# Second feed-forward product from split float32r operands, tail convolutions on VectorE

## The chip, the core and the metric

One core of a Trainium2 chip runs the whole program. The metric is the device time of one execution in microseconds, as the median of several runs. A profile of one execution shows what each engine does: TensorE (PE for its matmuls, PEld for its weight loads), VectorE (DVE), ScalarE (ACT), GpSimd (POOL) and the queue that issues DMAs (SP). "L538" is line 538 of the kernel before.

## The reference

Top-32 attention over 8 batches, 8 heads, 576 positions of 64 values, then a gated feed-forward net with 512 inputs, 1024 hidden channels and 512 outputs:

```python
scores = scale * np.matmul(q, k.transpose(0, 1, 3, 2))
kth = np.partition(scores, -top_k, axis=-1)[..., -top_k:-top_k + 1]
scores = np.where(scores >= kth, scores, -1000000000.0)
attn = softmax(scores)                      # over the last axis
x = np.matmul(attn, v)                      # heads side by side: (8, 576, 512)
h = np.maximum(x @ w_in, 0.0)
for k in range(3):
    conv_out += conv_w[k] * hp[:, k:k + S]  # along the positions, zero at the ends
gate = 1.0 / (1.0 + np.exp(-conv_out))
out = (h * gate) @ w_out
```

The weights arrive as 64-bit floats and are turned into 32-bit values on the chip.

## The kernel before

The attention is cut into 288 row tiles: 8 batches, 4 pairs of heads, 9 tiles of 128 rows each. A software pipeline runs one turn (`iteration`) per row tile, so a batch takes 36 turns. In a turn TensorE transposes the weights of an older tile (L304), does a share of the feed-forward work, computes scores of a new tile (L212, L217, L220) and the product with v (L335, L338). ScalarE takes the signs against the threshold (`sides`, L266), evacuates scores (L226) and transposes (L309) and takes exponentials into PSUM (`expo`, L278). VectorE looks for the 32nd largest score (L233, L253, L255, L281, L285) and weighs (L291). GpSimd multiplies scores with signs (`flip`, L271) and has the convolutions. Inside the loop the order of instructions on each engine is the order in which the program text emits them; behind the loop (the drain) a scheduler orders them.

The feed-forward net of a batch runs while the next batch attends. Its 576 positions are two parts, 256 and 320 rows. An `Expand` is one of 8 slices of 128 hidden channels of one part: 12 float32r matmuls (L400: high by high, high by low, low by high, for 4 slices of the input), a relu on ScalarE (L411), the convolution in two steps on GpSimd (`conv_a`, `conv_b`: L430, L439, L444), a tanh on ScalarE (L458), a gate on VectorE (L466). Each slice of hidden channels has a tile of its own (`g0_0` to `g1_7`). In the drain every second expansion of the last part has its convolution on VectorE (`conv_v`, L450).

A `Contract` is the second product of one block of up to 128 rows: 8 float32 matmuls of 512 columns with the gated activations as weights (L538), and for the last 64 rows of a batch 16 of 256 columns whose two halves go to different output partitions (L545). ScalarE copies the result to a tile `o` (L554, L557) and a DMA takes it out. The last five full blocks (the 320-row part of batch 6, and batch 7) instead use float32r: `halve` (L514 on ScalarE, L515 on VectorE) makes high and low parts of w_out and of the activations, and 24 float32r matmuls of 512 columns do the product (L534). Those pieces lie in `spare` and in tiles that the attention no longer needs.

A planner decides how much of it goes into a turn. `FEED` microseconds of planned TensorE time are added to a credit per turn, at most `PE_CAP`; `run_units` takes units from the two lanes, expansions first, until the credit is gone. A new expansion starts every `PACE` = 2 turns, and not while a contraction of the same part of an older batch is still queued. GpSimd tasks wait in a queue, `pool_tasks`, with planned costs and 2.0 us per turn.

At the start 33 blocks of weights are converted, one per turn: VectorE L148, L149, L159, ScalarE L153 to L155, GpSimd L164 and then L168 to L170 for w_in (which is split into a high and a low part) or L166 alone for w_out. Temporary tiles come from the tags of five groups of activation tiles.

## Time and profile before

| what | value |
|---|---|
| median of 3 runs | 1182.77 us (1179.51 to 1186.13) |
| the profiled execution | 1178.58 us, span 1176.8 us |
| TensorE | 1073.1 us busy, 91% of the span |
| VectorE | 1064.6 us, 90% |
| ScalarE | 973.8 us, 83% |
| GpSimd | 853.5 us, 73% |
| mean granted TensorE clock | 0.968 of full speed |
| chain of waits, by engine | TensorE 72%, VectorE 20%, ScalarE 5% |

Busy time is the union of an engine's instructions. A share of the whole span mixes three stages: a start in which weights are converted (to about 160 us), the loop, and the drain from about 1100 us. What a change is worth is read from the stage in which it lies. The chain of waits is followed back from the last instruction: each piece is what released the next one.

### The profile page before, as it was taken

How to read it: one execution, taken by the hardware profiler on the slowest of the kernel's cores; microseconds unless marked ns; L12 is line 12 of the kernel's file. 1: busy time of each engine (PE TensorE's matmuls, PEld its weight loads, DVE VectorE, ACT ScalarE, POOL GpSimd, SP SyncE). 2: the span in 40 equal slices, each digit the busy share in tenths (PEclk: the TensorE clock that was granted, in tenths of full speed). 3: DMA queues.
4: the chain of work that ended last, by engine and by line, in shares of the span. 5: the costliest groups of instructions: out<-in, count | busy, mean ns of one | idle time of the engine just before them, and what ended most of it. 6: DMA issues, size and time to landing. Idle time of an engine off the chain costs nothing.

```text
span 1176.8 us, 27192 instructions
## 1 busy us (share of the span) xinstructions
PE 1073.1 (91%) x7922; PEld 722.1 (61%) x7922; DVE 1064.6 (90%) x5823; ACT 973.8 (83%) x2295; POOL 853.5 (73%) x1147
## 2 busy tenths in 40 slices
PE   3666666889999999999999999999999999999997
PEld 1333444666666666666666665666666666666785
DVE  7999999999999999999999999999999999999451
ACT  5778888998988888898989888888988898898451
POOL 6776665778767786777767786877767886877770
PEclk9976689999999999999999999999999999999998
DMA  6230111111101111111110111111111011110001
GB/s 237 77 96 12 44 46 45 45 46 45 52 23 53 50 54 54 54 57 56 54 47 26 43 53 54 55 58 54 54 54 50 20 45 54 54 36 20 29 14 44
DMA packets 52095, 60.75 MB, mean 52 GB/s; under 512 B 9664, under 2 KB 31456, under 8 KB 51936
## 3 DMA queue, kind: packets, MB, share of 16 engines
q1 hardware_dynamic: 51936, 58.91, 15.9%
q8 instruction: 65, 1.06, 0.4%
q14 instruction: 94, 0.77, 0.2%
HBM read 49.31 MB, written 9.58 MB: 50 GB/s over the span
## 4 chain that ended last, share of the span: by engine, by line
PE 72%; DVE 20%; ACT 5%; POOL 1%; issue 1%; DMA 1%; SPq 0%; ACTq 0%; DVEq 0%; POOLq 0%
PE me L400 14%; PE mc L538 14%; PE s_ps L335 10%; PE pt L304 9%; PE s_ps L217 9%; DVE cand L233 5%; PE s_ps L220 3%; DVE e L291 3%; DVE z L281 3%; PE s_ps L212 3%; PE mc L545 2%; DVE cv L159 2%; PE s_ps L338 2%; DVE cand L255 1%; PE mc L534 1%; PE weights_ps L534 1%
## 5 line engine op out<-in xcount | busy, mean ns | idle before, releaser
L271 POOL TENSOR_TENSOR z<-rows,side 128x579 f32<-128x579 f32 x288 | 348.1, 1209 | 234.6 <-ACT side L266 217.4
L233 DVE MAX8 cand<-rows 128x8 f32<-128x82 f32 (+1 forms) x2016 | 453.0, 239 | 0.0
L278 ACT ACTIVATE weights_ps<-rows,z 128x576 f32<-128x576 f32 x288 | 219.6, 762 | 38.0 <-DVE e L291 29.7
L226 ACT COPY rows<-s_ps 128x576 f32<-128x576 f32 x288 | 183.0, 635 | 63.8 <-PE s_ps L338 41.9
L291 DVE SCALAR_TENSOR_TENSOR e<-rows,kth,weights_ps 128x576 f32<-128x576 f32 x288 | 230.6, 801 | 0.2
L266 ACT ACTIVATE side<-rows 128x576 bf16<-128x576 f32 x288 | 223.2, 775 | 0.9 <-DVE rows L253 0.7
L400 PE MATMUL me<-x_hi,wi 128*128 128x322 f32 (+1 forms) x928 | 220.1, 310 | 0.0
L281 DVE MAX8 z<-z 128x8 f32<-128x576 f32 x288 | 214.1, 744 | 0.0
L217 PE MATMUL s_ps<-k,q 64*128 64x512 f32 x512 | 157.8, 695 | 48.1 <-ACT xt L346 34.2
L304 PE MATMUL pt<-ident,e 128*128 128x128 f32 x1152 | 190.1, 290 | 10.9 <-DVE e L291 9.1
L538 PE MATMUL mc<-wo,g 128*128 128x512 f32 x416 | 198.8, 593 | 0.0
L335 PE MATMUL s_ps<-pT,vn 128*64 128x128 f32 (+1 forms) x2560 | 167.3, 275 | 17.5 <-ACT rows L226 17.5
L335 PEld LDWEIGHTS s_ps<-pT,vn 128*64 128x64 f32 x2560 | 131.0, 140 | 71.7 <-ACT rows L226 23.6
L400 PEld LDWEIGHTS me<-x_hi,wi 128*128 128x128 f32 x928 | 158.0, 190 | 0.9 <-issue 0.4
L304 PEld LDWEIGHTS pt<-ident,e 128*128 128x128 f32 x1152 | 134.1, 147 | 36.7 <-issue 19.4
L309 ACT COPY pT<-pt 128x512 f32<-128x512 f32 x256 | 151.5, 592 | 2.1 <-PE pt L304 2.1
L430 POOL TENSOR_SCALAR t<-g,cr 128x256 f32<-128x256 f32 (+1 forms) x248 | 129.7, 524 | 15.0 <-ACT g L411 13.9
L400 PE MATMUL me<-x_lo,wi 128*128 128x258 f32 (+1 forms) x464 | 137.7, 297 | 0.0
L253 DVE MAX8 rows<-cand 128x8 f32<-128x21 f32 x576 | 109.7, 190 | 0.0
L285 DVE SCALAR_TENSOR_TENSOR hot<-weights_ps,cnt,z 128x10 f32<-128x10 f32 x288 | 63.0, 219 | 49.6 <-ACT weights_ps L458 38.3
L444 POOL TENSOR_TENSOR t<-t,t 128x256 f32<-128x256 f32 (+1 forms) x124 | 99.8, 805 | 9.7
L220 PEld LDWEIGHTS s_ps<-k,q 128*128 128x128 f32 x256 | 40.9, 201 | 107.4 <-issue 107.4
(208 smaller groups left out, 1758.6 us busy)
## 6 DMA issues: line engine op xcount, KB each, us to landing
k<-in_k_dram SPq DMA_DIRECT2D x32, 352.0 KB
q<-in_q_dram SPq DMA_DIRECT2D x32, 288.0 KB
vn<-in_v_main_dram SPq DMA_DIRECT2D x32, 256.0 KB
rb<-row SPq DMA_DIRECT2D x64, 128.0 KB
out_dram<-o SPq DMA_DIRECT2D x32, 256.0 KB
raw<-in_w_in_dram SPq DMA_DIRECT2D x16, 256.0 KB
raw<-in_w_out_dram SPq DMA_DIRECT2D x16, 256.0 KB
vt<-in_v_tail_dram SPq DMA_DIRECT2D x32, 64.0 KB
```

What stands on the lines that cost most here:

```text
L217: nc.tensor.matmul(s_ps[:, 2 * h * BANK:(2 * h + 1) * BANK], lhsT=qx[d, at], rhs=kx[d, h * TAIL:h * TAIL + MAIN], start=True, stop=True)
L226: nc.scalar.copy(out=x, in_=s_ps[:, at:at + S])
L233: yield lambda c=c, at=at, n=n: nc.vector.max(out=t.cand[:, c:8 * CHUNKS:CHUNKS], in_=t.x[:, at:at + n])
L266: nc.scalar.activation(out=t.side[:, 2:S + 2], in_=t.x, func=AF.Sign, scale=-OVER, bias=t.row[:, 7:8], accum_out=t.cnt)
L271: nc.gpsimd.tensor_tensor(t.z[:, 8:S + 11], t.row[:, 6:S + 9], t.side, ALU.mult)
L278: nc.scalar.activation(out=e_ps, in_=t.x, func=AF.Exp, scale=scale, bias=t.shift)
L281: nc.vector.max(out=t.z[:, 0:8], in_=t.z[:, 10:S + 10])
L291: nc.vector.scalar_tensor_tensor(out=t.e, in0=t.x, scalar=kth[:, t.n:t.n + 1], in1=e_ps, op0=ALU.is_ge, op1=ALU.mult, accum_out=t.pc.sums[ ...
L304: nc.tensor.transpose(tp[:, i * P:(i + 1) * P], t.e[:, o + i * P:o + (i + 1) * P], ident)
L335: nc.tensor.matmul(a[r, 0:w], lhsT=st.pc.vn[:, h, i], rhs=st.pT[:, h if st.i < NI else 1 - h, i, 0:w], start=(i == 0), stop=False)
L400: nc.tensor.matmul(mm[:, 0:w], lhsT=wt, rhs=xx, start=(n == 0), stop=(n == len(ops) - 1))
L538: nc.tensor.matmul(mm, lhsT=h[:, at + self.s0:at + self.s0 + self.m], rhs=wo[:, f], start=(f == 0), stop=(f == NFT - 1))
```

## The change

Every block of the second product is now computed in float32r, from a high and a low part of both operands: high by high, high by low, low by high, 24 matmuls of 512 columns per block. w_out is split once, while it is converted. The activations are split per half row block (four hidden slices of 128 rows, 512 columns; for the last 64 rows all eight slices at once): a copy to float32r on ScalarE, and one turn later a subtraction on GpSimd; in the drain on VectorE at once. The 64-row blocks no longer use two halves of the output partitions. All slices of a part share one tile `g`. Three split buffers take the place of the conversion's scratch tile, which has three sets instead of five. An expansion waits until all older blocks of its part are split, instead of multiplied. In the drain all convolutions are on VectorE. One output tile instead of two; FEED 1.42 for 1.56, PE_CAP 1.6 for 1.8. The pieces, `spare` and `halve` are gone.

```diff
-PE_CAP = 1.8
-FEED = 1.56
+PE_CAP = 1.6
+FEED = 1.42
-OB = 2
+OB = 1
-SPARES = 6
+SPB = 3
...
-            self.tags = [f"g{k % 2}_{k // 2}" for k in range(i % 5 * 3, i % 5 * 3 + 3)]
+            if not scratch:
+                scratch.append(moe.tile([P, 4 * SPB, WB], F32, name="scratch", tag="split"))
+            self.at = i % SPB * 4
...
-                yield Convert(w_out[f * P:(f + 1) * P, n:n + WB], P, wo[:, f, n:n + WB], None)
+                yield Convert(w_out[f * P:(f + 1) * P, n:n + WB], P, wo[:, 0, f, n:n + WB], wo[:, 1, f, n:n + WB])
...
-            h = self.h = moe.tile([P, ROWS[self.part][1] - ROWS[self.part][0] + 4], F32, name=f"g{self.part}_{self.f}")
...
+            if self.f == 0:
+                g = self.gs["g"] = moe.tile([P, NFT, n + 4], F32, name=f"g{self.part}")
...
-            if self.b == B - 1 and self.part == 1 and self.f % 2 == 0 and not exact:
+            if state.it > NT + 4 and not exact:
                 self.conv_v()
...
-            self.count = NFT
-            self.cost = NFT * 4 * (DM if halves is None else DM // 2) / 2400
+            nf = NFT * TAIL // self.m
+            self.fs = range(half * nf, half * nf + nf)
+            self.first, self.final, self.ready = half == 0, self.fs[-1] == NFT - 1, False
+            self.count = nf
+            self.cost = nf * 3 * (DM / 2400 + 0.012)
+
+        def split(self):
...
+            both = extra[state.split % len(extra)] if late else parts[0][:, state.split % SPB]
+            self.hi, self.lo = (both[:, i].rearrange("p (f m) -> p f m", m=self.m) for i in range(2))
...
+            src = self.gs["g"][:, self.fs[0]:self.fs[-1] + 1, c0:c0 + self.m]
...
+            nc.scalar.copy(out=self.hi, in_=src)
+
+            def rest(engine):
+                engine.tensor_tensor(self.lo, src, f32(self.hi), ALU.subtract)
+                self.ready = True
+                unready.remove(self)
+
+            if state.it > NT + 4:
+                rest(nc.vector)
+            else:
+                pool_tasks.append((state.it + 1, 1.3, lambda: rest(nc.gpsimd)))
...
+            for i, f in enumerate(self.fs):
+                for n, (x, e) in enumerate(((self.hi, 0), (self.hi, 1), (self.lo, 0))):
+                    start, stop = f + n == 0, f == NFT - 1 and n == 2
+                    nc.tensor.matmul(mm[0:m], lhsT=x[:, i], rhs=wo[:, e, f], start=start, stop=stop)
                 yield self.cost / self.count
...
+    def split_next():
+        if not unready or blocks or fetched or cut or acted or dved:
+            return False
+        c = next((c for c in unready if not hasattr(c, "hi")), None)
+        if c is None or c.gs.get("done", 0) < NFT or (state.late_splits >= 4 if state.it > NT + 4 else state.splits >= SPB):
+            return False
+        c.split()
+        return True
...
-        if any(o.part == e.part and o.b < e.b for o in contracts) or (state.it < state.due and not tail):
-            return None
-        if contracted.cur is not None and contracted.unit.part == e.part and contracted.left > LEFT:
+        if any(o.part == e.part and o.b < e.b for o in unready) or (state.it < state.due and not tail):
             return None
...
-    for f in range(NFT):
-        pair = piece(), piece()
-        halve(wo[:, f], *pair)
-        wo2.append(pair)
-    for e in unsplit:
-        e.halve()
...
-    wo = const.tile([P, DF // P, DM], F32, name="wo")
+    wo = const.tile([P, 2, DF // P, DM], F32R, name="wo")
```

`split_next` is called once per turn, right behind the relus and output copies at the head of the turn (in the drain as often as it finds something).

## Rows read from the trace of the kernel before

**Rows 1.** The page, busy tenths in 40 equal slices of the span.
```profile
PE   3666666889999999999999999999999999999997
DVE  7999999999999999999999999999999999999451
```
**Rows 2.** Busy time by stage: one batch, and 14 us of the loop.
```profile
core 0: us, PE busy (x) PEld busy (x) DVE busy (x) ACT busy (x) POOL busy (x), PEclk, DMA share, GB/s
430.20:560.40 130.20, 129.53 (x982) 85.83 (x981) 122.19 (x707) 115.11 (x272) 98.35 (x132) 1.00 0.16 50
...
623.27:637.29 14.02, 14.02 (x104) 9.36 (x104) 13.94 (x84) 12.00 (x29) 12.68 (x19) 1.00 0.01 2
```
**Rows 3.** The chain of waits from 300 to 1000 us, shares by line.
```profile
by line: PE mc L538 20.1%; PE me L400 19.3%; PE s_ps L335 13.8%; PE pt L304 13.0%; PE s_ps L217 12.1%; PE s_ps L220 4.8%; PE s_ps L212 3.4%; PE s_ps L338 2.9%; PE mc L545 2.8%; PE me L317 1.8%; ACT rows L226 1.2%; ACT side L266 1.1%; issue 
```
**Rows 4.** Groups by line, 265 to 1070 us (busy, mean ns | idle before), and one wait.
```profile
L271 POOL TENSOR_TENSOR z<-rows,side 128x579 f32<-128x579 f32 x222 | 267.3, 1204 | 165.0 <-ACT side L266 164.0
L226 ACT COPY rows<-s_ps 128x576 f32<-128x576 f32 x222 | 141.7, 638 | 55.5 <-PE s_ps L338 36.9 <-PE s_ps L220 17.2
L285 DVE SCALAR_TENSOR_TENSOR hot<-weights_ps,cnt,z 128x10 f32<-128x10 f32 x221 | 48.8, 221 | 48.0 <-ACT weights_ps L458 38.1 <-ACT weights_ps L278 8.7
...
620.14 0.23 DVE L285 SCALAR_TENSOR_TENSOR hot<-weights_ps,cnt,z 128x10 f32<-128x10 f32 x1 [1.48 <-ACT weights_ps L458]
```
**Rows 5.** The chain in order of time: start us, us, what (merged).
```profile
269.07 2.58 PE mc L538 x6
...
1153.88 4.84 PE weights_ps L534 x21
...
1164.97 3.63 PE weights_ps L545 x32
```
**Rows 6.** Groups by line over the whole span, second product.
```profile
L538 PE MATMUL mc<-wo,g 128*128 128x512 f32 x416 | 198.8, 593 | 0.0
...
L545 PE MATMUL mc<-wo,g 128*64 128x256 f32 x224 | 28.6, 388 | 0.0
```
**Rows 7.** Copies on ScalarE (timeline, group) and subtractions on GpSimd (groups).
```profile
1092.00 2.18 ACT L514 CAST rows<-wo 128x512 fp32r<-128x512 f32 x4 [0.30 <-DVE e L291]
...
L554 ACT COPY o<-mc 128x512 f32<-128x512 f32 x29 | 17.1, 589 | 11.0 <-PE mc L534 10.9
...
L372 POOL TENSOR_TENSOR x_lo<-xt,x_hi 128x576 fp32r<-128x576 f32 x32 | 45.5, 1423 | 1.7
...
L439 POOL TENSOR_TENSOR t<-t,g 128x320 f32<-128x320 f32 x60 | 45.8, 763 | 4.8
```
**Rows 8.** Start: ns min/median/max with first and last start; two steps from the timeline.
```profile
L169 POOL TENSOR_SCALAR wi<-cv x16: 404/404/418, 12.1 to 80.2; 128x256 fp32r<-128x256 f32 x16
L170 POOL TENSOR_TENSOR wi<-cv,wi x16: 723/728/731, 12.6 to 80.7; 128x256 fp32r<-128x256 f32 x16
...
L291 DVE SCALAR_TENSOR_TENSOR e<-rows,kth,weights_ps x11: 800/802/804, 29.0 to 77.5; 128x576 f32<-128x576 f32 x11
...
L291 DVE SCALAR_TENSOR_TENSOR e<-rows,kth,weights_ps x15: 798/801/808, 87.9 to 156.0; 128x576 f32<-128x576 f32 x15
...
97.70 0.41 DVE L159 SCALAR_TENSOR_TENSOR cv<-raw,cv 128x256 uint16<-128x256 uint16 x1
...
102.02 1.04 DVE L159 SCALAR_TENSOR_TENSOR cv<-raw,cv 128x256 uint16<-128x256 uint16 x1
...
L515 DVE TENSOR_TENSOR spare<-wo,spare x3: 667/679/687, 96.0 to 114.9; 128x512 fp32r<-128x512 f32 x3
```
**Rows 9.** Loop end and drain: busy time by stage, and two instructions from the timeline.
```profile
1050.00:1100.00 50.00, 47.98 (x359) 33.72 (x358) 46.48 (x204) 41.23 (x102) 42.26 (x60) 1.00 0.06 18
1105.00:1160.00 55.00, 55.00 (x328) 47.88 (x327) 21.81 (x40) 21.80 (x53) 33.97 (x58) 1.00 0.07 23
...
1081.25 0.63 PE L304 MATMUL pt<-ident,e 128*128 128x128 f32 x4 [0.88 <-DVE rows L253]
...
1147.27 0.55 DVE L450 SCALAR_TENSOR_TENSOR t<-g,cr 128x320 f32<-128x320 f32 x1 [0.59 <-ACT g L411]
```

More of the change, by code (lines that the diff above doesn't have):

```diff
@@ L124, in corner @@
         return s_ps[:, BANK + TAIL + i * P:BANK + TAIL + i * P + w]
+    scratch = []
     class Convert:
@@ L376, in attend_and_feed @@
     class Expand:
+        final = True
         def __init__(self, b, part, f, gs):
@@ L475, in gated @@
         def gated(self):
-            self.gs[self.f] = (self.h, self.at)
+            self.gs["done"] = self.gs.get("done", 0) + 1
             state.flying -= 1
-            if late(self.b, self.part):
-                if wo2:
-                    self.halve()
-                else:
-                    unsplit.append(self)
-        def halve(self):
-            n = NI * TAIL
-            pair = self.b, self.part, self.f // 2
-            if pair not in halves:
-                halves[pair] = [piece(), piece()]
-            parts = [p[:, self.f % 2 * n:(self.f % 2 + 1) * n] for p in halves[pair]]
-            halve(self.h[:, self.at:self.at + n], *parts)
-            self.gs[self.f] += tuple(parts)
@@ L505, in attend_and_feed, with __init__ @@
-    scraps, halves, wo2, unsplit = pieces(), {}, [], []
-    def late(b, part):
-        return b + part >= B - 1
-    def piece():
-        return next(scraps)
-    def halve(src, hi, lo):
-        nc.scalar.copy(out=hi, in_=src)
-        nc.vector.tensor_tensor(lo, src, f32(hi), ALU.subtract)
     class Contract:
-        def __init__(self, b, part, s0, halves, gs):
-            self.b, self.part, self.s0, self.halves, self.gs = b, part, s0, halves, gs
+        def __init__(self, b, part, s0, half, gs, box):
+            self.b, self.part, self.s0, self.gs, self.box = b, part, s0, gs, box
@@ L527, in pieces @@
         def pieces(self):
-            w = DM // 2
-            mm = self.mm = next(contract_banks)() if state.it > NT + 4 else bank("mc")
-            if self.halves is None:
-                for f in range(NFT if late(self.b, self.part) else 0):
-                    hi, lo = (p[:, self.s0:self.s0 + P] for p in self.gs[f][2:])
-                    for n, (a, e) in enumerate(((hi, 0), (hi, 1), (lo, 0))):
-                        nc.tensor.matmul(mm, lhsT=a, rhs=wo2[f][e], start=(f + n == 0), stop=(f == NFT - 1 and n == 2))
-                    yield self.cost / self.count
-                for f in range(0 if late(self.b, self.part) else NFT):
-                    h, at = self.gs[f][0:2]
-                    nc.tensor.matmul(mm, lhsT=h[:, at + self.s0:at + self.s0 + self.m], rhs=wo[:, f],
-                                     start=(f == 0), stop=(f == NFT - 1))
-                    yield self.cost / self.count
-                return
@@ L542, in pieces @@
-            for f in range(NFT):
-                h, at = self.gs[f][0:2]
-                for n, half in enumerate(self.halves):
-                    nc.tensor.matmul(mm[n * TAIL:n * TAIL + self.m, 0:w], lhsT=h[:, at + self.s0:at + self.s0 + self.m],
-                                     rhs=wo[:, f, half * w:(half + 1) * w], start=(f == 0), stop=(f == NFT - 1))
+            if self.first:
+                self.box.mm = next(contract_banks)() if state.it > NT + 4 else bank("mc")
+            mm, m = self.box.mm, self.m
@@ new lines, in emit @@
+            nc.scalar.copy(out=o[0:m], in_=mm[0:m])
+            nc.sync.dma_start(out=out[self.b, r:r + m, :], in_=o[0:m])
+    parts, extra, outs_late, unready = [], [], [], []
+    def split_next():
[6 more added lines that the diff above has]
+        return True
@@ L564, in ffn @@
         for s0 in range(0, n, P):
-            contracts.append(Contract(b, part, s0, (0, 1) if n - s0 == TAIL else None, gs))
+            box = Box()
+            units = [Contract(b, part, s0, half, gs, box) for half in range(1 if n - s0 == TAIL else 2)]
+            contracts.extend(units)
+            unready.extend(units)
     expand_banks = cycle([lambda: e_mm, lambda: bank("pt"), lambda: s_ps[:, 0:BANK], lambda: s_ps[:, 2 * BANK:3 * BANK]])
@@ L583, in next_contract @@
     def next_contract():
-        if not contracts or contracted.waiting >= (2 if state.it > NT + 4 else CB) or blocks or fetched or cut or acted or dved:
+        if not contracts or not contracts[0].ready:
             return None
-        c = contracts[0]
-        if len(c.gs) < NFT or (c.halves is None and late(c.b, c.part) and not wo2):
-            return None
-        contracted.waiting += 1
+        if contracts[0].first:
+            if contracted.waiting >= (2 if state.it > NT + 4 else CB):
+                return None
+            contracted.waiting += 1
         return contracts.popleft()
@@ L690, in iteration @@
                 lane.finished.popleft().emit()
+        while split_next() and it > NT + 4:
+            pass
         avs, av_next = av_next, []
```

72 lines of the change are left out of this document (39 added, 33 removed).

## The prediction

> **What bounds the kernel now.** I read the page first, then the busy time of each engine batch by batch, then the chain of waits, then the groups by line. The page's slices show VectorE full and TensorE waiting at the start, both full in the loop, and TensorE alone full at the end [rows 1]; only the stages tell them apart. In the loop one batch (36 row tiles) takes 130.2 us, and of these TensorE is busy 129.5, VectorE 122, ScalarE 115, GpSimd 98 [rows 2]; the other five batches lie within 0.3 us of that, save the last for VectorE. TensorE idles 0.7 us a batch, VectorE 8. The chain of waits of this stretch runs over TensorE lines, the second product (L538) first with 20.1% [rows 3]. VectorE's idle time stands in front of L285, where it waits for ScalarE [rows 4]: it runs ahead and is held back. So a microsecond taken from TensorE counts in the loop, until VectorE is next at 122. In the drain, from 1105 us on, TensorE is busy throughout [rows 9].
>
> A matmul's record ends later than the next one starts, so I price matmuls by the chain, which counts start to start. By the Trainium skill (Perfetto Trace Analysis, Identifying the Most-Contended Engine) matmul busy time is a poor measure and the busy share of weight loads is the better one; that is 86 of 130 us here, and the most contended engine would be VectorE, so that the loop would gain nothing. It is the second rival below; for the forecast I side with the chain.
>
> **Second product, full blocks of 128 rows.** Before: 16 records for 8 float32 products; 6 records take 2.58 us, 0.43 each, a block 6.88 us [rows 5]. After: 24 float32r matmuls of 512 columns. The trace has the same form, in the drain (L534): 21 in 4.84 us, 0.2305 each, so 5.53 us a block [rows 5]. Gain 1.35 us. L538 has 416 records [rows 6], so 26 blocks: −35.1 us. Five blocks are split already and keep their price.
>
> **Second product, the 64-row tails.** Before, the two halves of the columns go to different output partitions and run together: 32 records take 3.63 us [rows 5], half of a full block. After, 24 matmuls of 512 columns for 64 rows; columns set the price, so again 5.53, a loss of 1.90. L545 has 224 records in one bank [rows 6] and these 32 in the other, 8 tails: +15.2 us. TensorE's sum is −19.9 us; per loop batch −4 × 1.35 + 1.90 = −3.5, so 129.5 becomes 126.0.
>
> **Splitting the activations** adds 9 half-block copies on ScalarE and 9 subtractions on GpSimd per batch. Four copies of 128x512 to float32r in a row took 2.18 us, 0.55 each [rows 7]: 4.9 us; the tail's output copy is now 512 columns wide, 0.59 us [rows 7], where it was 256, which I take as 0.2 more. ScalarE goes from 115.1 to 120.2. A subtraction of 512 columns lies between 0.76 (320 columns) and 1.42 us (576) [rows 7]; by columns 1.26, so GpSimd goes from 98 to about 110. VectorE stays at 122. All three stay below 126, closely. The copy stands at the head of ScalarE's turn and waits for gates that VectorE ran a turn earlier, before the weighing that ScalarE's exponential already waits for; so it waits for nothing new. Behind it queue the side signs (L266) and the evacuation of scores (L226), which now idles 55 us for TensorE over 222 tiles [rows 4] and so takes in most of a 0.55 us delay. The subtraction stands before a flip (L271) at worst, and GpSimd idles 165 us there [rows 4]. The product waits for the subtraction; three split buffers let two be ready ahead. With one output buffer the copy to it waits for the transfer before, which went out at least four turns (14 us) earlier. These edits cost nothing while that slack lasts; without it 57 copies in the loop (9 for each of 6.3 batches) would cost 31 us.
>
> **The loop's new period.** Its least is 126.0 + 0.7 = 126.7 and its most 130.2, where the other engines hold it. VectorE's share rises from 94 to 96%, ScalarE's from 88 to 94, GpSimd's from 75 to 86, so waits will meet more often. I take 127.5, near the lower end, since in 14 us of the loop TensorE idled not at all with VectorE at 13.94, ScalarE at 12.0 and GpSimd at 12.7 [rows 2], about the shares that I expect. The 0.8 us over the least, 6.3 batches long: +5.0 us.
>
> **The planner.** One batch costs it 54.5 us now (16 expansions 23.8, four blocks of 6.83, tail 3.4) of 36 × 1.56 = 56.2; after, 23.8 + 40 × 0.676 = 50.8 of 36 × 1.42 = 51.1. The reserve falls from 1.7 to 0.3 us a batch. What the first batches are late by, since a split needs a turn on ScalarE and one on GpSimd first, isn't made up: I count about three half blocks (3 × 2.77 = 8.3 us) more left for the drain. Where TensorE is the bound that only moves work; what is missing before 300 us, beside VectorE, is lost: +2 us (0 to 5).
>
> **Start.** The low parts of w_out add two GpSimd steps to 16 blocks, 0.40 and 0.73 us [rows 8], and VectorE paces the start. There VectorE's two-input step L159 took 0.41 us beside a nearly free GpSimd and 1.04 beside a busy one [rows 8]. The price shows in the turns: with the steps of w_in (the same four) 10 turns from 29.0 to 77.5 us, 4.85 each; with those of w_out 14 turns from 87.9 to 156.0, less three L515 halvings of 0.68, 4.72 each [rows 8]. So 16 × 0.13 = +2 us, and the halvings, which the change removes, −2: nothing. Three scratch buffers instead of five suffice, since a block lives for three turns. By the Trainium skill (SBUF — State Buffer, Who interferes with whom) a VectorE instruction with two SBUF inputs and a GpSimd one that reads SBUF block each other entirely; at full length that would be 16 × 1.13 = 18 us, and the trace's turns show 2.
>
> **Loop end.** The other halvings of w_out and of the late activations run among the last turns and hold TensorE, 0.88 us behind VectorE at the longest place; in 1050 to 1100 us it misses 2.0 us [rows 9]. I take all of it as gone (0 to 2): −2.
>
> **Drain.** TensorE stays the bound: its work only grows by two tails, counted above. VectorE takes the convolutions, 0.55 us a step [rows 9], and with a gate of about that 1.65 us for each of 16 expansions; with 9 subtractions as long as the halvings (0.68) [rows 8] that is 33 of about 80 us, so it keeps up. The halves must be complete before they are split, and buffers are four: +1.5 us. The last copy is wider: +0.2.
>
> **Sum:** −19.9 + 5.0 + 2 + 0 − 2 + 1.5 + 0.2 = −13.2 us. The profiled execution took 1178.6 us, the span and 1.8 around it; the median of the runs is 1182.8, 0.36% above. I take the sum from the median: 1169 us.
>
> **Rivals.** First, half of the loop's gain is lost to waits: ScalarE's copies fall into turns that hold a tanh, a relu and an output copy too. The period is then 128.9, 6.3 × 1.4 = 8.8 us more: 1178, within the noise. For it speaks that three engines stand at 86 to 96%; against it that each runs ahead of TensorE by part of a turn.
>
> Second, slower: the 8 us that VectorE waits per batch are not slack but a loop of their own, weighing, exponential, tanh (L458), L285, weighing [rows 4]. It decides once that loop and VectorE's 122 us cannot be done in under 130 us. Then the period stays 130.2, TensorE idles instead, the two tails of the drain cost 3.8, the work left over 8.3, with +1.5 and −2: 1194. For it speaks that the longest such wait is 1.48 us [rows 4] and follows from a tanh in a crowded turn; against it that the chain passes TensorE [rows 3] and that in those 14 us VectorE ran at 99% [rows 2].
>
> Third, the start pays the full 18 us: 1187, no change by the bound below. Against it the two periods above.
>
> **How the numbers follow.** Forecast 1169 (1157 to 1176) 0.67; half lost 0.15; VectorE's loop 0.13; start 0.05. Below 1157 all waits would have to vanish (−19.9 − 2 − 2, and the start free). The range 1157 to 1187 leaves out the slower rival and little else. A measurement of this kernel can tell about 0.5%, 6 us, from no change: faster 0.67, same 0.20, slower 0.13.
>
> **What would show it.** The period of a batch falls from 130.2 to about 127.5 with TensorE busy 126; if it is under 127 or over 129, the waits were mis-sized. In the loop 24 records of the second product take 5.5 us, for tails as well. The chain stays on TensorE; a chain that changes to VectorE's L285 or ScalarE's L266 is the second rival. Turns at the start stay at 4.85 us for w_out. The drain grows by some 12 us, work carried over and tails. Wrong would be, above all, float32r matmuls dearer in the loop than in the drain, or TensorE idle at the head of second products, waiting for GpSimd.

## The result and the profile after

| what | before | after |
|---|---|---|
| median | 1182.38 us, 4 runs | 1167.59 us, 4 runs (1165.43 to 1172.38) |
| ratio after to before | | 0.988, 95% interval 0.984 to 0.992 |
| profiled execution, span | 1176.8 us | 1167.0 us |
| the 73rd weighing starts at | 312.4 us | 316.6 us |
| from there the next 180 turns (five batches) | 653.8 us | 633.5 us |
| the last 35 turns | 125.0 us | 120.3 us |
| last weighing to the end | 85.7 us | 96.6 us |

The change is faster by 1.2%, 14.8 us; 1169 was forecast. The four lower rows come from the start times of the weighing (L291 before, L293 after; one per turn) in the timelines; they add up to the span. In the profiled pair the change lost 4.2 us in the first 73 turns, won 20.3 in five batches and 4.7 in the last turns, and gave 10.9 back in the drain. That is 9.8 us together; the medians differ by more, since the profiled execution of before was a fast one (1178.6 us) and that of after was slower than its median.

The page of after: busy time and share of each engine; busy tenths in 40 slices and the granted clock; the chain by engine.
```profile
PE 1056.8 (91%) x8066; PEld 775.1 (66%) x8066; DVE 1066.8 (91%) x5832; ACT 997.6 (85%) x2335; POOL 896.1 (77%) x1072
...
PE   3665676888999999999999999999999999999996
...
DVE  7999989999999999999999999999999999998550
...
PEclk9867659999999999999999999999999999999999
...
PE 47%; DVE 42%; ACT 9%; issue 1%; DMA 0%; SPq 0%; POOL 0%; ACTq 0%; POOLq 0%
```
Against [rows 1] VectorE's row has a dent in the sixth slice, while the clock's row stands at 6 and 5 of ten in the fifth and sixth: that is the start, below. TensorE has 72% of the chain before and 47% now; of the rest VectorE has taken most (20% to 42%), ScalarE some (5% to 9%).

Busy time by stage of after: three batches, the drain, and the five batches as a whole; behind them the five batches of before.
```profile
core 0: us, PE busy (x) PEld busy (x) DVE busy (x) ACT busy (x) POOL busy (x), PEclk, DMA share, GB/s
441.80:568.20 126.40, 124.71 (x1000) 92.22 (x1000) 121.48 (x706) 118.24 (x276) 104.86 (x123) 1.00 0.16 52
568.20:696.20 128.00, 126.35 (x1005) 92.35 (x1004) 122.16 (x707) 120.89 (x283) 109.15 (x128) 1.00 0.16 51
696.20:822.80 126.60, 126.05 (x1007) 92.96 (x1004) 121.86 (x708) 119.69 (x280) 108.58 (x129) 1.00 0.16 51
...
1070.40:1167.00 96.60, 87.66 (x513) 73.64 (x509) 41.27 (x83) 33.58 (x74) 13.45 (x17) 0.98 0.09 29
...
316.60:950.10 633.50, 627.00 (x5014) 462.54 (x5013) 609.20 (x3531) 596.99 (x1394) 539.06 (x632) 1.00 0.16 51
```
```profile
312.40:966.10 653.70, 650.08 (x4921) 431.18 (x4921) 613.11 (x3531) 578.20 (x1352) 493.71 (x660) 1.00 0.16 50
```
From weighing to weighing a batch took 130.8 us (653.8 / 5; the stretch of [rows 2] is cut half a microsecond short of a period) and takes 126.7 (633.5 / 5). TensorE's busy time per batch fell from 130.0 to 125.4, so it idles 0.7 us a batch before and 1.3 after; VectorE's stayed; ScalarE's rose by some 4 to 119.4 and GpSimd's by 9 to 107.8. In the drain TensorE has 88 us of work in 97, the rest being the last output's way out.

Part of the shorter period is work put off. Five batches hold 600 matmul records of the second product (24 for each of 25 blocks) and 960 of the first; those of after hold 585 (L536) and 948 (L404), some 5 us less, and the missing ones come in the drain. In the last two of the five, which hold all of theirs, a batch takes 126.6 and 127.3 us, with TensorE busy 126.0 and 126.4.

The chain of waits of after from 300 to 1000 us, shares by line.
```profile
by line: PE mc L536 13.8%; PE me L404 11.0%; DVE cand L235 8.9%; PE s_ps L337 8.7%; PE pt L306 8.6%; PE s_ps L219 8.4%; DVE e L293 7.0%; DVE z L283 4.2%; PE s_ps L222 3.3%; ACT weights_ps L280 2.8%; PE s_ps L214 2.7%; DVE cand L257 2.2%; AC
```
In [rows 3] VectorE's lines did not come up. Now its searches (L235), its weighing (L293) and L283 carry a fifth: the chain passes VectorE in some turns and TensorE in others.

Groups of after by line, 265 to 1070 us (busy, mean ns | idle before, releasers).
```profile
L273 POOL TENSOR_TENSOR z<-rows,side 128x579 f32<-128x579 f32 x229 | 276.2, 1206 | 96.8 <-ACT side L268 84.5 <-issue 6.0 <-POOL split L517 3.5
...
L228 ACT COPY rows<-s_ps 128x576 f32<-128x576 f32 x225 | 143.8, 639 | 28.9 <-PE s_ps L340 18.3 <-PE s_ps L222 6.3
...
L517 POOL TENSOR_TENSOR split<-g,split 128x512 fp32r<-128x512 f32 x56 | 66.1, 1182 | 0.0
...
L287 DVE SCALAR_TENSOR_TENSOR hot<-weights_ps,cnt,z 128x10 f32<-128x10 f32 x229 | 49.7, 217 | 30.1 <-ACT weights_ps L465 19.9 <-ACT weights_ps L280 8.6
...
L514 ACT CAST split<-g 128x512 fp32r<-128x512 f32 x57 | 35.9, 630 | 0.1
```
The three idle times of [rows 4] have all shrunk: GpSimd ahead of the flip from 165 to 97 us, ScalarE ahead of the evacuation from 55.5 to 29, VectorE ahead of L287 (L285 before) from 48 to 30. The slack that should hide the new copies and subtractions was drawn on, and was not used up.

The chain of after in order of time, second product (start us, us, what).
```profile
343.70 2.09 PE mc L536 x9
...
1136.12 5.48 PE weights_ps L536 x24
1141.60 5.47 PE mc L536 x24
1147.07 5.47 PE weights_ps L536 x24
1152.54 5.54 PE mc L536 x24
```
The last is a 64-row tail. A block takes 5.5 us, in the loop (2.09 / 9 = 0.232 us a matmul) as in the drain (0.228).

### The profile page after: what moved, and what is told of

Read it like the earlier page. It is cut to its first block, busy times and chain, and to the rows that moved or that the text cites. A ratio compares the mean times of both kernels' runs of the same rounds, so it can differ in the third digit from the quotient of the medians.

```text
span 1167.0 us, 27441 instructions
## 1 busy us (share of the span) xinstructions
PE 1056.8 (91%) x8066; PEld 775.1 (66%) x8066; DVE 1066.8 (91%) x5832; ACT 997.6 (85%) x2335; POOL 896.1 (77%) x1072
## 4 chain that ended last, share of the span: by engine, by line
PE 47%; DVE 42%; ACT 9%; issue 1%; DMA 0%; SPq 0%; POOL 0%; ACTq 0%; POOLq 0%
DVE cand L235 12%; PE mc L536 12%; DVE e L293 9%; PE me L404 8%; PE s_ps L337 6%; DVE z L283 6%; PE pt L306 6%; PE s_ps L219 5%; DVE cand L257 3%; DVE scratch L161 2%; ACT weights_ps L280 2%; PE s_ps L222 2%; DVE rows L255 2%; DVE hot L287 2%; PE weights_ps L536 2%; PE s_ps L214 2%
## 5 line engine op out<-in xcount | busy, mean ns | idle before, releaser
L235 DVE MAX8 cand<-rows 128x8 f32<-128x82 f32 (+1 forms) x2016 | 451.5, 238 | 0.1
L280 ACT ACTIVATE weights_ps<-rows,z 128x576 f32<-128x576 f32 x288 | 219.7, 763 | 41.4 <-DVE e L293 31.5
L293 DVE SCALAR_TENSOR_TENSOR e<-rows,kth,weights_ps 128x576 f32<-128x576 f32 x288 | 230.3, 800 | 0.3
L404 PE MATMUL me<-x_hi,wi 128*128 128x322 f32 (+1 forms) x928 | 220.8, 310 | 1.2 <-ACT g L418 1.2
L283 DVE MAX8 z<-z 128x8 f32<-128x576 f32 x288 | 213.8, 742 | 0.0
L536 PE MATMUL mc<-wo,split 128*128 128x512 f32 (+1 forms) x756 | 205.1, 404 | 0.0
L219 PE MATMUL s_ps<-k,q 64*128 64x512 f32 x512 | 154.3, 680 | 51.2 <-ACT xt L348 36.7
L337 PE MATMUL s_ps<-pT,vn 128*64 128x128 f32 (+1 forms) x2560 | 171.2, 279 | 17.1 <-ACT rows L228 16.9
L337 PEld LDWEIGHTS s_ps<-pT,vn 128*64 128x64 f32 x2560 | 134.3, 143 | 54.0 <-ACT rows L228 25.7
L404 PEld LDWEIGHTS me<-x_hi,wi 128*128 128x128 f32 x928 | 157.5, 189 | 2.3 <-ACT g L418 1.9
L536 PEld LDWEIGHTS mc<-wo,split 128*128 128x128 f32 (+1 forms) x756 | 126.5, 179 | 26.5 <-ACT o L552 0.2
L404 PE MATMUL me<-x_lo,wi 128*128 128x258 f32 (+1 forms) x464 | 138.8, 299 | 0.0
L437 POOL TENSOR_SCALAR t<-g,cr 128x256 f32<-128x256 f32 (+1 forms) x222 | 113.5, 511 | 0.0
L219 PEld LDWEIGHTS s_ps<-k,q 64*128 64x128 f32 x512 | 40.4, 193 | 83.8 <-ACT xt L348 47.5
```

Of the source, the lines that this page charges most:

```text
L219: nc.tensor.matmul(s_ps[:, 2 * h * BANK:(2 * h + 1) * BANK], lhsT=qx[d, at], rhs=kx[d, h * TAIL:h * TAIL + MAIN], start=True, stop=True)
L235: yield lambda c=c, at=at, n=n: nc.vector.max(out=t.cand[:, c:8 * CHUNKS:CHUNKS], in_=t.x[:, at:at + n])
L280: nc.scalar.activation(out=e_ps, in_=t.x, func=AF.Exp, scale=scale, bias=t.shift)
L283: nc.vector.max(out=t.z[:, 0:8], in_=t.z[:, 10:S + 10])
L293: nc.vector.scalar_tensor_tensor(out=t.e, in0=t.x, scalar=kth[:, t.n:t.n + 1], in1=e_ps, op0=ALU.is_ge, op1=ALU.mult, accum_out=t.pc.sums[ ...
L337: nc.tensor.matmul(a[r, 0:w], lhsT=st.pc.vn[:, h, i], rhs=st.pT[:, h if st.i < NI else 1 - h, i, 0:w], start=(i == 0), stop=False)
```

## Experiments

All start from the changed kernel. Single executions of one program differ by some 7 us (1165.4 to 1172.4 for after), so small effects are read from the turns. This table, from the weighings' start times and the spans, holds all runs (us):

| kernel | 13th to 27th | 27th to 37th | 73rd at | five batches | last 35 turns | drain | span |
|---|---|---|---|---|---|---|---|
| before | 68.08 | 32.65 | 312.4 | 653.8 | 125.0 | 85.7 | 1176.8 |
| after | 69.58 | 36.00 | 316.6 | 633.5 | 120.3 | 96.6 | 1167.0 |
| e0_same | 69.53 | 32.51 | 314.6 | 633.4 | 120.3 | 95.8 | 1164.2 |
| e2_two_terms | 69.53 | 35.90 | 319.5 | 623.2 | 118.2 | 72.7 | 1133.6 |
| e3_copy_twice | 69.53 | 33.32 | 318.3 | 652.4 | 124.2 | 95.1 | 1190.0 |
| e4_vector_sub | 69.51 | 34.72 | 317.1 | 656.9 | 122.7 | 91.0 | 1187.7 |
| e5_sub_twice | 69.61 | 32.73 | 313.9 | 634.8 | 121.3 | 95.8 | 1165.9 |
| e6_start_no_low | 67.96 | 35.75 | 314.3 | 633.6 | 120.3 | 95.7 | 1163.9 |
| e8_pool_conv | 69.52 | 35.95 | 319.9 | 633.4 | 120.3 | 95.9 | 1169.5 |
| e9_copy_late | 69.54 | 36.12 | 316.8 | 631.3 | 120.6 | 96.0 | 1164.6 |
| e10_merged_tails | 69.53 | 35.81 | 320.2 | 628.6 | 118.3 | 90.1 | 1157.3 |
| e12_pool_copy | 69.57 | 32.49 | 314.3 | 629.0 | 118.2 | 103.8 | 1165.3 |
| e13_merged_pool_copy | 69.53 | 33.50 | 314.3 | 629.6 | 119.0 | 97.6 | 1160.5 |

**e0_same: no edit.**

> The changed kernel once more, to see how much of the start's loss is its own. In its first profile the first 36 turns ended 5.9 us later than before the change: about 2.5 us in turns that convert w_out, 3.4 us in two turns at 165 to 175 us in which TensorE was granted half its clock. If the clock's recovery is chance, the second part moves or goes here (spread of some 3 us) and the batch periods stay at 126.7 on average, within 0.5; if both belong to the change, the turns 26 to 30 again lose 3 us.

1165.98 us. Five batches, last turns and 13th to 27th weighing repeat to 0.1 us, the drain to 0.8; but the 27th to 37th weighing take 32.5 us for 36.0. The loop's figures can be read from one execution; those of the first 73 turns can't. The expectation of chance holds.

**e2_two_terms: what bounds the loop.** The edit drops one of three terms, and a third of the planned cost:
```diff
-self.cost = nf * 3 * (DM / 2400 + 0.012)
+self.cost = nf * 2 * (DM / 2400 + 0.012)
...
-for n, (x, e) in enumerate(((self.hi, 0), (self.hi, 1), (self.lo, 0))):
+for n, (x, e) in enumerate(((self.hi, 0), (self.hi, 1))):
```


> Leaves out the low-by-high product of the second feed-forward product (16 instead of 24 matmuls a block); splits and subtractions stay. TensorE's work falls by 5 x 8 x 0.2305 = 9.2 us a batch, to about 117. Theory A (TensorE bounds the loop, VectorE's 122 us are next, its waits are slack): the period falls from 126.7 to 123 to 124, VectorE above 98%. Theory B (VectorE's loop through exponential and tanh holds the period): it stays at 126 to 127, and only the drain gets shorter, by some 9 us for the last batch.

1135.48 us. One batch of it, and the chain from 300 to 1000 us:
```profile
444.10:568.70 124.60, 117.58 (x970) 86.69 (x969) 121.40 (x708) 119.04 (x280) 108.13 (x128) 1.00 0.17 52
```
```profile
by line: DVE cand L235 12.6%; PE me L404 9.2%; DVE e L293 8.7%; DVE z L283 7.8%; PE mc L536 6.2%; PE s_ps L337 5.6%; PE s_ps L219 5.5%; PE pt L306 5.3%; ACT weights_ps L280 3.8%; DVE cand L257 3.6%; ACT side L268 3.3%; ACT rows L228 3.1%; i
```
With 7.8 us less of TensorE per batch (125.4 to 117.6) the period falls by only 2.1, to 124.6, and TensorE now idles 7 us a batch: the loop's next bound is VectorE's turn, at 124.6 and not at VectorE's busy 121.4. That is nearer to theory A, though its 123 to 124 was too low. In the drain, where TensorE is alone, all of the missing work counts: 138 second-product records instead of 240, and 73 us instead of 96. So the changed kernel's 126.7 lies a little above two bounds at once, TensorE's work (125.4) and VectorE's turn (124.6).

**e3_copy_twice, e4_vector_sub, e5_sub_twice: has each engine slack for its new work?** e3 issues ScalarE's split copy twice, e5 GpSimd's subtraction twice, e4 makes the loop's subtraction on VectorE, ahead of its gates.
```diff
 nc.scalar.copy(out=self.hi, in_=src)
+nc.scalar.copy(out=self.hi, in_=src)                              # e3
...
-pool_tasks.append((state.it + 1, 1.3, lambda: rest(nc.gpsimd)))
+rests.append(lambda: rest(nc.vector))                             # e4
...
 engine.tensor_tensor(self.lo, src, f32(self.hi), ALU.subtract)
+if engine is nc.gpsimd:                                           # e5
+    engine.tensor_tensor(self.lo, src, f32(self.hi), ALU.subtract)
```


> The split's copy on ScalarE is issued twice, to the same place: 9 x 0.55 = 4.9 us more a batch, ScalarE from 119.6 to 124.5 of 126.7. Theory A (copies lie in ScalarE's waits for TensorE): most is hidden, the period rises by less than 1.5 us, the total by less than 9. Theory C (the copies stand on the path at the head of a turn): the period rises by 4 to 5, the total by about 30.

> The subtraction is put on VectorE in the loop too, ahead of the gates: 9 x 0.69 = 6.2 us a batch move from GpSimd (which had 1.18 us each) to VectorE, 122 to 128. Theory A, with VectorE next in line: the period rises to 128.5 to 130, the total by 12 to 20 us. If VectorE has real slack (TensorE alone decides): the period stays within 1 us of 126.7.

> The GpSimd subtraction of each split in the loop is issued twice, about 9 x 1.18 = 10.6 us of GpSimd more per batch (107.5 busy of 126.7 before). Theory A (GpSimd has slack: the flip of a turn waits for ScalarE's sign, and the subtraction lies behind it or fits before): period of a batch within 0.5 of 126.7, whole time 1164 to 1171. Theory B (every subtraction delays a flip, and the flip delays VectorE's turn): period 128 to 130, time 1172 to 1185. What it would say of the change: the single subtraction costs about as much as the second one.

1191.76, 1189.49 and 1167.69 us. The first is nearest to theory C, the second lies above theory A (131.4 us a batch for 128.5 to 130), and the third is theory A's. Over five batches, 45 half blocks, against e0: e3 +19.0 us for 45 × 0.63 = 28 us more of ScalarE, e4 +23.5 for 45 × 0.78 = 35 more of VectorE, e5 +1.4 for 45 × 1.18 = 53 more of GpSimd. GpSimd's slack is real. A second copy and a subtraction on VectorE both cost two thirds of their length. Of e3 one batch and the chain from 300 to 1000 us; then VectorE's wait over the five batches of e0 and of e3:
```profile
577.00:708.80 131.80, 126.88 (x1006) 92.31 (x1005) 122.38 (x708) 125.81 (x292) 108.99 (x128) 1.00 0.16 50
```
```profile
by line: DVE cand L235 13.9%; DVE e L293 11.2%; ACT weights_ps L280 7.0%; DVE z L283 6.5%; ACT side L268 5.0%; ACT pT L311 5.0%; PE mc L537 4.6%; ACT rows L228 4.4%; PE me L404 3.9%; DVE cand L257 3.4%; PE s_ps L337 3.2%; PE s_ps L219 3.1%;
```
```profile
L287 DVE SCALAR_TENSOR_TENSOR hot<-weights_ps,cnt,z 128x10 f32<-128x10 f32 x180 | 39.2, 218 | 22.7 <-ACT weights_ps L465 15.4 <-ACT weights_ps L280 6.2
L287 DVE SCALAR_TENSOR_TENSOR hot<-weights_ps,cnt,z 128x10 f32<-128x10 f32 x180 | 39.5, 219 | 39.6 <-ACT weights_ps L465 21.6 <-ACT weights_ps L280 16.6
```
VectorE's wait for exponential (L280) and tanh (L465) goes from 22.7 to 39.6 us: 17 of the 19.0 us by which five batches became longer. No engine is full here, ScalarE 125.8 and TensorE 126.9 of 131.8, and the chain now runs over VectorE and ScalarE lines ahead of TensorE's. By this chain and the releasers of that wait the loop weighing, exponential, tanh, L287, the one of the prediction's second rival, now sets the turn in most places. The split copies lie in it: the two of e3 (L514, L515) hold this chain for 27 of the 700 us, the one of after for 4. In e4 VectorE itself is late, by waits for ScalarE's copy too (265 to 1095 us):
```profile
L517 DVE TENSOR_TENSOR split<-g,split 128x512 fp32r<-128x512 f32 x58 | 45.0, 776 | 10.7 <-ACT split L514 10.7
```

**e9_copy_late and e12_pool_copy: does the single copy cost too?** e9 moves the call of `split_next` behind the sign, the evacuation and the transposed copies; e12 gives the loop's copy to GpSimd. First the edit of e9, then that of e12:
```diff
-        while split_next() and it > NT + 4:
-            pass
...
             if st.i == NI:
                 norm_wait.append((it + NORM_LAG, st.pc))
+
+        while split_next() and it > NT + 4:
+            pass
```
```diff
-nc.scalar.copy(out=self.hi, in_=src)
+if late:
+    nc.scalar.copy(out=self.hi, in_=src)
...
 def rest(engine):
+    if not self.late:
+        nc.gpsimd.tensor_scalar(self.hi, src, 1.0, 0.0, ALU.mult, ALU.add)
     engine.tensor_tensor(self.lo, src, f32(self.hi), ALU.subtract)
...
-    pool_tasks.append((state.it + 1, 1.3, lambda: rest(nc.gpsimd)))
+    pool_tasks.append((state.it + 1, 1.95, lambda: rest(nc.gpsimd)))
```


> The split's ScalarE copy is issued later in its turn: behind the sign, the evacuation and the transposed copies and ahead of the exponential, instead of ahead of the sign. Doubling the copy cost 3.9 us per batch (period 130.6 for 126.7). Theory A (ScalarE's total sets that price, since its exponential and tanh end the loop that runs through VectorE): same place in the sum, period within 0.5 of 126.7. Theory B (the place sets it: ahead of the sign it delays sign, flip and evacuation): period 125 to 126, time 1156 to 1164. Theory C (ahead of the exponential it lies straight on the loop weigh, exponential, tanh, hot): period over 127.5.

> The split's copy in the loop is made by GpSimd, right ahead of its subtraction, instead of by ScalarE; in the drain it stays on ScalarE. About 9 x 0.63 = 5.7 us of ScalarE less per batch, about as much more on GpSimd, where 10.6 us more cost 0.3 us per batch. Theory A (TensorE bounds the batch at 126 of 126.7 us, ScalarE only catches up when the copy is doubled): period 126.0 to 126.7, time within 4 us of the changed kernel. Theory B (the single copy already costs like the second one, 3.9 us per batch): TensorE's own 126.0 stops the gain, so period 126.0, but VectorE's wait ahead of the L287 operation (27.4 us over 265 to 1070) goes under 10. Theory C (GpSimd becomes late, and its flip with it): period over 128.

1166.45 and 1167.19 us. Another place wins 2.1 us in five batches, 0.4 a batch: the place in the turn hardly matters (theory A). Without the copy ScalarE has 115.5 us a batch and five batches are 4.4 us shorter, the last turns 2.1, but the drain is 8.0 longer. Two stages of e12, a batch and the drain, and the chain from 300 to 1000 us:
```profile
core 0: us, PE busy (x) PEld busy (x) DVE busy (x) ACT busy (x) POOL busy (x), PEclk, DMA share, GB/s
691.70:817.80 126.10, 125.07 (x998) 91.72 (x998) 121.60 (x708) 115.52 (x270) 112.08 (x134) 1.00 0.16 52
...
1061.47:1165.00 103.53, 95.68 (x567) 80.80 (x565) 46.42 (x93) 37.76 (x82) 15.34 (x20) 0.99 0.09 29
```
```profile
by line: PE me L404 16.4%; PE mc L539 15.4%; PE s_ps L337 11.1%; PE s_ps L219 10.9%; PE pt L306 10.7%; PE s_ps L222 4.3%; DVE cand L235 4.2%; PE s_ps L214 3.5%; DVE e L293 3.2%; PE s_ps L340 2.3%; DVE z L283 2.2%; ACT rows L228 1.8%; ACT we
```
TensorE's busy time per batch fell with the period, and 567 matmul records instead of 513 are left for the drain. The turns are shorter because they hold less, not because a wait is gone (VectorE's wait ahead of L287 is 26 us, for 30). The copy does show in the chain: without it VectorE's three lines have 10% instead of 20. But TensorE idles no less, 18.5 us from the 73rd weighing to the end, for 16.7 in e0. So the single copy costs nothing that shows in the whole time, as far as a run can tell that moves the copy to GpSimd and does not take it away. Theory A holds there; its period (126.0 to 126.7) was 0.2 us too high. It is the second copy that goes past the slack.

**e6_start_no_low: the start.**
```diff
-yield Convert(w_out[f * P:(f + 1) * P, n:n + WB], P, wo[:, 0, f, n:n + WB], wo[:, 1, f, n:n + WB])
+yield Convert(w_out[f * P:(f + 1) * P, n:n + WB], P, wo[:, 0, f, n:n + WB], None)
...
+nc.gpsimd.memset(wo[:, 1].bitcast(F32), 0.0)
```


> Leaves out the low part of w_out: it is set to zero once, and the start's twelve subtractions for it are not made, so the output lacks the product with that part; the number of matmuls is the same. Theory A (what the start lost against the kernel before, 5.9 us by turn 36, is GpSimd's added subtractions holding up VectorE): the 36th weigh comes 3.5 to 6 us earlier than the 191 to 195 us of the changed kernel. Theory B (the loss comes from TensorE's granted clock of 0.5 between 150 and 170 us, or from the batch's first feed-forward work, and not from these subtractions): the 36th weigh within 1 us of 191 to 195. Whole time 1162 to 1166 by A, 1165 to 1169 by B.

1165.65 us. The edit leaves out both added steps of all 16 blocks. The 37th weighing starts at 192.8 us, within theory B's range; but each theory is right for another stretch. The 14 turns with w_out's blocks take 67.96 us for 69.51 to 69.61 in all other runs: GpSimd's two steps per block cost 1.6 us, and they cost it through VectorE's step L161 (L159 before). It is shown in these turns, of before, after and e6:
```profile
L159 DVE SCALAR_TENSOR_TENSOR cv<-raw,cv 128x256 uint16<-128x256 uint16 x15 | 12.4, 825 | 0.0
```
```profile
L161 DVE SCALAR_TENSOR_TENSOR scratch<-raw,scratch 128x256 uint16<-128x256 uint16 x15 | 15.4, 1029 | 0.0
```
```profile
L161 DVE SCALAR_TENSOR_TENSOR scratch<-raw,scratch 128x256 uint16<-128x256 uint16 x15 | 14.1, 938 | 0.0
```
The step takes 15 × 0.09 = 1.4 us more in after than in e6. But in e6 it already takes 15 × 0.11 = 1.7 us more than in before, though GpSimd has the same steps there (14 of 0.82 and 14 of 0.67 us in both): with the three halvings gone, 2.0 us of VectorE, the turns became no shorter, 67.96 for 68.08. The timelines show why, here of before, e6 and after in the same turn:
```profile
95.99 0.67 DVE L515 TENSOR_TENSOR spare<-wo,spare 128x512 fp32r<-128x512 f32 x1
96.63 1.20 POOL L271 TENSOR_TENSOR z<-rows,side 128x579 f32<-128x579 f32 x1 [0.92 <-ACT side L266]
97.70 0.41 DVE L159 SCALAR_TENSOR_TENSOR cv<-raw,cv 128x256 uint16<-128x256 uint16 x1
```
```profile
97.82 1.20 POOL L273 TENSOR_TENSOR z<-rows,side 128x579 f32<-128x579 f32 x1 [0.98 <-ACT side L268]
98.23 1.07 DVE L161 SCALAR_TENSOR_TENSOR scratch<-raw,scratch 128x256 uint16<-128x256 uint16 x1
```
```profile
98.01 1.21 POOL L273 TENSOR_TENSOR z<-rows,side 128x579 f32<-128x579 f32 x1
98.15 1.35 DVE L161 SCALAR_TENSOR_TENSOR scratch<-raw,scratch 128x256 uint16<-128x256 uint16 x1
```
The step ends 0.28 us after the flip that runs when it starts. Of its 45 executions in the three traces 36 start inside a flip; 35 of them last the rest of that flip and 0.28 us, one with 0.06 us of flip left takes 0.40, and the nine that start outside take 0.40 to 0.41. In before the halving filled time in which the step would have waited for the flip. In after the flip starts later, straight behind GpSimd's added steps (its idle time ahead of the flips of these turns falls from 22.3 to 7.0 us), so the step meets more of it.

The ten turns behind that take 35.75 us in e6, 36.00 in after and 32.51 in e0, the same program. Two stretches of after, and the same of e0:
```profile
160.00:170.00 10.00, 8.48 (x40) 4.85 (x42) 8.49 (x53) 7.50 (x18) 5.24 (x7) 0.50 0.09 26
170.00:180.00 10.00, 7.88 (x70) 5.05 (x68) 8.22 (x49) 7.62 (x19) 5.52 (x5) 0.86 0.33 104
```
```profile
160.00:170.00 10.00, 6.80 (x69) 4.24 (x69) 10.00 (x64) 8.76 (x23) 6.69 (x8) 1.00 0.15 36
170.00:180.00 10.00, 7.74 (x70) 5.17 (x70) 10.00 (x60) 8.99 (x21) 7.00 (x6) 1.00 0.27 95
```
In after the granted clock of TensorE is 0.50 (1.2 GHz) from 160 to 170 us, TensorE is busy 85% and VectorE falls to 85%; in e0 the clock is 1.00 (2.4 GHz) and VectorE is full. So 3.5 of the 5.9 us by which after's 37th weighing is later than before's (194.6 for 188.7 us) lie in a stretch that differs from execution to execution.

**e8_pool_conv: the drain.**
```diff
-if state.it > NT + 4 and not exact:
+if self.b == B - 1 and self.part == 1 and self.f % 2 == 0 and not exact:
     self.conv_v()
```


> The convolutions after the last attention turn go back to GpSimd as in the kernel before (of the last part every second one on VectorE), the rest as in the changed kernel. Theory A (the drain is TensorE's: PE is full there, so it does not matter who makes the convolutions): time from the last weigh to the end within 1 us of the changed kernel's 96.6. Theory B (GpSimd's convolutions would hold up the drain, and VectorE took them off the path): 2 to 8 us more.

1171.30 us, but the drain takes 95.9 us with GpSimd's convolutions, as in e0 (95.8). Theory A: VectorE's part of the change moves nothing, TensorE is the drain's bound. What the run is slower by lies ahead of the stretch that the edit changes: ten slow turns as in after, and its 73rd weighing at 319.9 us.

**e10_merged_tails and e13_merged_pool_copy: taking out what the change added.** The tails now cost as much as full blocks. e10 keeps the 64 tail rows of an even batch and multiplies them together with those of the next batch, one block of 128 rows; e13 also moves the loop's copies to GpSimd as e12 does.
```diff
+class Keep:
+    def split(self):
+        c0 = self.gs["at"] + self.s0
+        nc.scalar.copy(out=kept_tail[0], in_=self.gs["g"][:, :, c0:c0 + TAIL])
...
+            if tail and b % 2 == 0 and b < B - 1:
+                unready.append(Keep(b, part, s0, gs))
+                continue
...
+            halves = [(slice(self.m - n, self.m), self.gs["g"][:, fs, c0:c0 + n])]
+            if self.both:
+                halves.append((slice(0, TAIL), kept_tail[0][:, fs]))
...
+            for cols, src in halves:
+                nc.scalar.copy(out=self.hi[:, :, cols], in_=src)
```


> Aims at the tail blocks, whose split product takes 5.53 us for 64 rows as for 128: the 64 tail rows of an even batch are kept (one more ScalarE copy) and multiplied together with those of the next, so four tail products in place of eight, 22 us of TensorE less, 2.76 per batch. Theory A (TensorE bounds the loop down to where VectorE holds it, at the 124.6 us that the run with two terms showed): period 124.6 to 125.2, 9 to 13 us off the loop, and up to 5 off the drain: 1150 to 1158. Theory B (ScalarE's exponential and tanh hold the loop near 126 already, as the doubled copy suggests): period 126 to 126.7, time 1160 to 1166.

> Both of these edits: tails of two batches in one product, and the loop's split copies on GpSimd. Theory A (TensorE, then VectorE): no further than the merged tails alone, period 124.6 to 125.2, time within 2 us of that run. Theory B (with TensorE at 123.3 us per batch, ScalarE's copies are what holds VectorE's turn, so that 124.6 was no limit of VectorE's own 121.9): period 123.3 to 124.3, 3 to 8 us better than the merged tails alone.

e10: 1152.48 us median of 5 runs (1151.68 to 1159.07), ratio to before 0.975, interval 0.973 to 0.978: better than both kernels. e13: 1162.45 us (4 runs), 0.985 (0.981 to 0.988). Two batches and the drain of e10:
```profile
core 0: us, PE busy (x) PEld busy (x) DVE busy (x) ACT busy (x) POOL busy (x), PEclk, DMA share, GB/s
444.80:570.50 125.70, 123.74 (x1001) 92.75 (x1001) 121.78 (x708) 119.29 (x283) 109.95 (x132) 1.00 0.16 51
570.50:695.20 124.70, 120.82 (x982) 89.85 (x981) 121.06 (x706) 118.27 (x277) 104.91 (x123) 1.00 0.16 51
...
1067.16:1157.00 89.84, 81.68 (x491) 71.46 (x487) 41.35 (x85) 33.85 (x76) 14.39 (x17) 0.97 0.09 32
```
The median falls by 15 of the 22 us that TensorE has less. In the profiled pair five batches give 4.9 us, the last turns 2.0 and the drain 6.5, and the start takes 3.6 back. The time is theory A's, the period, 125.7 on average, lies between the two: in the first four batches those with a merged tail product (123.7 us of TensorE) and those without (120.8) alternate, and the latter end at 124.6 and 124.8, near VectorE's 124.6 of e2; why the fifth takes 127.9 is open. For e13 neither theory holds: the period is the same (125.9) and the drain is 7.5 us longer, as in e12; 540 matmul records are left for it instead of 491, and second products now wait for GpSimd, if only 2.2 us in all (265 to 1045 us):
```profile
L546 PE MATMUL mc<-wo,split 128*128 128x512 f32 x633 | 173.9, 407 | 2.3 <-POOL split L526 1.6 <-POOL split L527 0.6
```

## Why the prediction was right

The forecast was 1169 (1182.8 − 13.2 is 1169.6), the median 1167.6, and the mechanism was the one given: a microsecond off TensorE counts in the loop until VectorE ends the turn. From the 73rd weighing to the end the profiled pair gains 14.1 us: TensorE is busy 16.6 us less and idles 2.5 more. The sum had −19.9 and 4.7 for this (5.0 − 2 + 1.5 + 0.2), but some 4 us of the −19.9 belong to matmuls ahead of the 73rd weighing (22 records of the second product before, 24 cheaper ones after), where VectorE is full. Two terms came out otherwise than put, the start and the loop's end.

- **Second product, −19.9 us: right.** 5.47 to 5.54 us a block against 5.53, tails too, and no dearer in the loop. In a batch with all of its work TensorE's busy time fell from 130.0 to 126.0 and 126.4, for −3.5 in the sum. Six full blocks, not five, had the form already (32 less the 26 counted); the sum does not use that number.
- **The copies and subtractions: right in the whole time, for a narrower reason than given.** 0.63 us for an estimated 0.55, 1.18 for 1.26; the engines' totals (VectorE 121.8, ScalarE 119.4, GpSimd 107.8) came within 2.5 us of those worked out. That there is room for one copy is what e12 shows in the whole time. But the slack of ScalarE was not the 29 to 55 us that it idles ahead of the evacuation: the doubled copy cost two thirds of its length while ScalarE idled 6 us a batch.
- **The loop's new period: 127.5 forecast, 126.7 on average, for another reason than fewer waits.** Under 127 was to show that the waits were mis-sized. The waits nearly came: TensorE's idle time rose from 0.7 to 1.3 us a batch, 0.6 for the 0.8 of the term, 2.9 us over five batches. What is shorter is the work, by the 15 and 12 records that these batches put off; the two batches that hold all of theirs took 126.6 and 127.3. In e2 VectorE's turn takes 124.6. The prediction put VectorE's bound at 122; it is 121.4 of work and some 3 us of waits for exponential and tanh. The chain, which was to stay on TensorE, went to VectorE for a fifth.
- **The start: mis-sized, 0 for +5.9 us by the 37th weighing in the profiled pair.** By the 73rd it is +4.2, and +2.2 in e0, where the planner's term had 2. 1.0 us arose before w_out's turns. In these 14 turns the price of GpSimd's steps was put at 2 us, from the w_in turns, and is 1.6 (e6): right. The gain of the vanished halvings was put at 2 us and is 0.1: the time that they took is now spent waiting for the flip. The remaining 3.4 us are the stretch at low clock, which e0 shows not to belong to the change, and which no term of the sum could hold. Whether the change makes this clock likelier is open: the one profile of before has the low clock too, 0.50 from 145 to 150 us, but is back at 0.97 from 160 to 170, and single executions of before, without a profile kept, had mean clocks from 0.957 (1185.1 and 1185.3 us) to 0.976 (1180.0 us). The reading that L159 took 0.41 us beside a nearly free GpSimd was wrong: GpSimd was busy throughout that step, with 0.13 us of the flip left.
- **Loop end, −2: it did not come.** From 1040 to 1070 us TensorE still idles 1.8 us, behind ScalarE's relu (1.2) and one attention copy (0.6) instead of the halvings; over the last 35 turns it idles 1.9 us before and 2.2 after. These turns won 4.7 us, all of it less work of TensorE.
- **The drain: right.** Some 12 us more were expected, 10.9 came. Ten blocks of the second product are left for it, where before it had 6.6 and two tails: 1.4 blocks more, 7.6 us for the 8.3 of the planner's three half blocks, and 3.8 for the tails. TensorE does them without a gap. That VectorE's convolutions would not matter was right (e8).
- **The rivals.** Half the gain lost, 128.9: not so. VectorE's loop through the tanh: it exists, as e3 shows, but it ends at 124.6 and not at 130; it does not hold the period while ScalarE has 119 us a batch, and does with 124. The 18 us for the start: 1.6 of them. By the Trainium skill (SBUF — State Buffer, Who interferes with whom) a VectorE instruction with two SBUF inputs contends with a GpSimd one that reads SBUF, for ports that one holds at a time. The trace agrees for L161, which ends 0.28 us after the flip. But the price is the rest of the one flip that the step meets, not the length of all that GpSimd does: a tenth of the added 16 × 1.13 us. The Trainium skill (Perfetto Trace Analysis, Identifying the Most-Contended Engine) judges TensorE by the share of its peak rate and by its weight loads; the prediction read it by the weight loads alone, and so the loop would have stayed unchanged. Their busy time rose from 86.2 to 92.5 us a batch while the batch became 4.1 us shorter, so here the chain was the better guide.

How close 1169 came to 1167.6 is partly luck. The profiled pair gained 9.8 us, e0 against the same profile of before 12.6 and the medians 14.8, for 13.2 in the sum; executions of one program scatter by more than these differ, most of it in the start.

## What to carry over

Price an engine's slack by the chain it stands in, not by its idle time: doubling one added instruction tells at once whether there is room, and GpSimd had it where ScalarE had one copy's worth. Where TensorE bounds loop and drain alike, a shorter period may only move work to the drain (e12, and a part of the change itself), so count the matmuls of a stretch and read both ends before a gain is believed. When a form makes small blocks as dear as full ones, put two small blocks together: that was worth as much again as the change itself.

## What the runs showed of the hardware

- The granted clock of TensorE was 0.5 (1.2 GHz) in stretches between 140 and 175 us, where TensorE is busy 50 to 85% of the time, and came back to 1.00 (2.4 GHz) at some 158 us in one execution (e0) and after 170 in another of the same program. The ten turns there take 32.5 or up to 36.1 us. Another such place lies from 200 to 210 us: granted clock 1.00 with VectorE full in e0, 0.83 with VectorE busy 83% in e8, and 123.3 and 125.3 us for the 36 turns around it.
- 24 float32r matmuls of 512 columns take 5.5 us for 64 rows as for 128; the float32 form took 3.63 us for 64 rows in two halves of the output partitions, for 6.88 a full block [rows 5].
- VectorE's two-input step L161 (L159 before) took 0.40 us when no flip of GpSimd ran at its start, and else the rest of that flip and 0.28 us: 0.83 on average before, 0.94 in e6 beside the same GpSimd steps, and 1.03 beside two more per block. Taking 2.0 us of other work from VectorE ahead of it gained 0.1.
- GpSimd was busy 9.8 us more per batch for 0.3 us of period (e5), while ScalarE's 4.9 more cost 3.8 (e3), at busy shares of 85 and 94% before the addition.
